# A linear attention and gated MLP kernel: turned queries on GpSimd's DMA queue, the verdict by a product with ones

## The chip, the cores and the metric

The kernel runs on one core of a Trainium2 chip. The core has five engines with a queue of instructions each: TensorE (PE, with its weight loads shown apart as PEld), VectorE (DVE), ScalarE (ACT), GpSimd (POOL) and SyncE (SP), and 16 DMA engines that serve the transfers which SP, ScalarE or GpSimd issue. The metric is the device time of one execution in microseconds; lower is better.

## What is computed

The reference is a gated linear recurrence over 768 steps for 4 batches of 8 heads (head size 48), followed by an MLP whose activation is h·cos(h):

```python
def _attn_ref(q, k, v, a_re, a_im):
    mag = np.sqrt(a_re * a_re + a_im * a_im)
    scale = np.minimum(mag, 0.999) / (mag + 1e-06)
    a_re_n, a_im_n = (a_re * scale, a_im * scale)
    for t in range(S):
        ar, ai = (a_re_n[:, :, t, :, None], a_im_n[:, :, t, :, None])
        new_re = ar * S_re - ai * S_im
        new_im = ar * S_im + ai * S_re
        kv = np.einsum('bhd,bhe->bhde', k[:, :, t], v[:, :, t])
        S_re, S_im = (new_re + kv, new_im)
        y[:, :, t] = np.einsum('bhd,bhde->bhe', q[:, :, t], S_re)

def _moe_ref(x, w_in, w_out):
    h = x @ w_in
    g = h * np.cos(h)
    return (g @ w_out).astype(np.float32)
```

Between the two, the attention output is rearranged to 3072 tokens of 384 numbers; w_in is 384x2048 and w_out 2048x384.

## The kernel before

The 768 steps of a batch are cut into chunks of 128; two chunks make a group, and there are 12 groups. There are two programs in one kernel. `fast_path` assumes things that its data may break (for example decays that stay in a range, gate arguments that a table can take), and keeps records of them in three small tiles, `least`, `odd` and `wide`. At the end `verdict` turns these records into one number, `flag`. Every engine reads the flag and branches: in one arm `general_path` computes everything again, in the other only the last piece of the output is stored (`late["store"]`, issued by ScalarE).

In a group of the fast path, logarithms, powers, phases and sines of the decays come first. `g_stack` (L909) multiplies keys and queries by cosine and sine and stacks both products into `ks` and `qs`; four VectorE multiplies, keys first. `f_transpose` (L921) then turns the stacks so that the head's numbers lie on partitions: VectorE transposes blocks of 32 into `tr`, SP stores `tr` to DRAM (`moved`), and SP loads it back in another order, keys as `kT` in four transfers, queries as `qT` in one. The chunk's scores (`sc`, from kT and qT) are masked into `atm`, its outputs (`yp`) go through DRAM once more to become `xT`, and the MLP follows: `hp` is xT times w_in, ScalarE and VectorE make `gate` from it, and the second product is done in seven half-sized products instead of eight (`products`, with sums in `sum` and `op`; `seventh`, L1160, evicts each one into `ot`, the last group's last quarter into `rest`).

The order of the work is written out by hand up to group 2; after it `weave` (L1213) merges lists of steps by position numbers between 0 and 1, one body for each of groups 2 to 11: products of the group before, scores and outputs of this group, the decays, phases and `keys` of the next group, and `first`, the 96 `hp` matmuls of this group, at the end. The next group's keys and queries are turned while these matmuls run, and its scores stand right behind them on TensorE. TensorE's and GpSimd's instructions are each tied into one chain in the order in which they are written (`chain`); the other queues are ordered by the tile framework from these positions.

GpSimd does little: it loads weights, and from group 4's body on (`guarded`) it waits with a one-element copy (`wait_for`, L1277) for the last gate of the group before, and then loads two pieces of the raw weights again, into one buffer, for VectorE and ScalarE to look at (`guard`, L645).

In the last body `judged` advances the verdict in three steps. The first (L1610 to L1624) reduces the three records on VectorE and writes the two results to DRAM as one line, which SP loads back into one partition; the second (L1626 on) takes the minimum of that line, compares, and has all engines read the flag; the third only fixes TensorE's place.

Of the kernel before, what the change touches and what calls it, by code (L numbers as in the profile page):

```python
# [11 lines left out]
F32 = mybir.dt.float32  # L12
# [475 lines left out]
def fast_path(ctx, tc, q, k, v, a_re, a_im, moe_w_in, moe_w_out, out, least, odd, wide,  # L488
# [417 lines left out]
        special(out=sn, in_=ph, func=AF.Sin, scale=TWO_PI)  # L906
        special(out=cs, in_=cs, func=AF.Sin, scale=-TWO_PI, bias=half_pi_b)

    def g_stack(g, i, n):  # L909
        x = X[g]  # L910
        if i == 0:
            for name in "ks", "qs":
                x[name] = gt.tile([C, G * H, 2, D], F32, tag=name, name=name)
        for name, product in ("ks", "Q"), ("qs", "mag"):
            for a, trig in enumerate(("cos", "sin")):
                vector.tensor_tensor(
                    out=x[name][:, ds(i * H, n * H), a],
                    in0=cut(x[product], i, n).rearrange("p (x d) -> p x d", d=D),
                    in1=cut(x[trig], i, n).rearrange("p (x d) -> p x d", d=D), op=ALU.mult)

    def f_transpose(g, i, n, name):  # L921


        if i == 0:
            X[g][name] = ft.tile([D2, G * H, Q4, 32] if name == "kT" else [D2, Q4, G * H, 32], F32,
                                 tag=name, name=name, bufs=1)
        tr = ft.tile([C, NB, n * H, 32], F32, tag="tr", name="tr")
        turn = vector.transpose(out=tr, in_=X[g][name[0] + "s"][:, ds(i * H, n * H)].rearrange(
            "p x a d -> p x (a d)").rearrange("p x (r b) -> p b x r", b=NB))
        if name == "qT" and "gated" in X[g - 1]:  # L930
            behind(turn, X[g - 1]["gated"])
        moved = rows_d.tile([Q4, D2, n * H, 32], F32, tag="moved", name="moved", bufs=3)
        nc.sync.dma_start(out=moved.rearrange("q (r b) x j -> (q r) b x j", b=NB), in_=tr)
        if name == "kT":
            for q4 in range(Q4):
                nc.sync.dma_start(out=X[g][name][:, ds(i * H, n * H), q4], in_=moved[q4])
        else:
            nc.sync.dma_start(out=X[g][name][:, :, ds(i * H, n * H)],
                              in_=moved.rearrange("q c x j -> c q x j"))

    def f_turn(g, i, name, hh):

# [217 lines left out]
    def seventh(g, p, part):  # L1160


        x, name = X[g], SEVEN[p]
        if p == 0 and part == 0:
            x["sum"] = pm.tile([C, E2], F32, tag="acc", name="sum", bufs=1)
            x["ot"] = [msb.tile([C, DM], F32, tag="ot", name="ot") for _ in range(G)]

        alone = g == NG - 1 and p == 6
        summed = p in (0, 3, 5, 6) and not alone
        if not summed and part == 0:  # L1170
            x["op"] = pm.tile([C, E2], F32, tag="m", name="op", bufs=2)
        ps = x["sum"] if summed else x["op"]
        for j in range(part * HJ // 2, (part + 1) * HJ // 2):
            matmul(ps, lhsT=left(g, name, j), rhs=right[name][:, j],
                   start=(j == 0 and (p == 0 or not summed)),
                   stop=(j == HJ - 1), skip_group_check=summed)
        if part == 0:
            return
        c11, c12, c21, c22 = (x["ot"][i][:, ts(half, E2)] for i in range(2) for half in range(2))
        if g == NG - 1:  # L1180
            c12 = rest
        if p in (0, 3, 5) or p == 6 and not alone:
            late["scalar"] = scalar.mul(out={0: c11, 3: c21, 5: c22, 6: c12}[p], in_=ps, mul=scale)
        if g == NG - 1 and p == 5:
            scalar.mul(out=c12, in_=ps, mul=scale)
        for part_ in {1: [c11], 2: [c21], 4: [c21, c22], 6: [c12] * alone}.get(p, []):
            added = vector.scalar_tensor_tensor(out=part_, in0=ps, scalar=scale,
                                                in1=part_, op0=ALU.mult, op1=ALU.add)
            if alone:
                behind(added, late["read DVE"])  # L1190
            late["vector"] = added
        row = g * G * C
        if g == NG - 1 and p == 1:
            behind(nc.sync.dma_start(out=out[ds(row, C), 0:E2], in_=c11), late["line"])
        elif p == 4:
            put = nc.sync.dma_start(out=out[ds(row + C, C), :], in_=x["ot"][1])
            if g == NG - 1:
                behind(put, late["read SP"])
        elif p == 6 and alone:
            late["store"] = lambda: nc.scalar.dma_start(out=out[ds(row, C), E2:DM], in_=c12)  # L1200
        elif p == 6:
            nc.sync.dma_start(out=out[ds(row, C), :], in_=x["ot"][0])
# [7 lines left out]
    def mixes(g, lo, hi):  # L1210
        return [lambda p=p: mixed(g, p) for p in range(lo, hi)] if g >= PLAIN else []
# [14 lines left out]
    def keys(g):  # L1226

        if not 0 <= g < NG:
            return
        for i, n in spans(g):  # L1230
            yield lambda i=i, n=n: g_trig(g, i, n)
            yield lambda i=i, n=n: (g_stack(g, i, n), p_end(g, i, n))
            for name in "kT", "qT":
                if g >= PEG:
                    yield lambda i=i, n=n, name=name: f_transpose(g, i, n, name)

    def turned(g, i, name):
        return [lambda hh=hh: f_turn(g, i, name, hh) for hh in range(2)]
# [329 lines left out]
    for n in range(2, NG):  # L1568
        weave((mixes(n - 1, 2, 4), 0.0, 0.12), (logs(n + 1), 0.0, 0.02), (chunks(n), 0.0, 0.36),
              (upper[2:] if n == 2 else [], 0.0, 0.2), (products(n - 1, 0, 2 + (n < NG - 1)), 0.0, 0.36),  # L1570
              (prods(n + 1), 0.25, 0.27), (second(n - 1, 1), 0.36, 0.5),
              (products(n - 1, 2 + (n < NG - 1), 7), 0.4, 0.56),
              (phases(n + 1), *((0.472, 0.476) if n == PLAIN else (0.516, 0.524))),
              (keys(n + 1), *((0.5, 0.62) if n == PLAIN else (0.53, 0.64))),
              (last_quarter() if n == PLAIN else [], 0.9, 1.0), (first(n), 0.56, 1.0),
              (mixes(n, 0, 2), 0.9, 1.0), (guarded(n - 1, per) if n > 3 else [], 0.1, 0.9))
    checked = verdict(late, temp)

    def judged():
        late["tensor"] = tail["tensor"]  # L1580
        next(checked, None)

    weave((mixes(NG - 1, 2, 4), 0.0, 0.1), ([judged], 0.05, 0.15),
          (products(NG - 1, 0, 7), 0.0, 1.0), ([judged], 0.58, 0.6), ([judged], 0.76, 0.8))
    assert not guards
    return late
@with_exitstack
def kernel(ctx, tc, q, k, v, a_re, a_im, moe_w_in, moe_w_out, out):
# [16 lines left out]
        tc.add_manual_dep(ins.ins, other.ins.name, mybir.DependencyInfo(  # L1605
            mybir.DependencyClass.NoSync, mybir.DependencyReason.DATA))

    def verdict(late, temp):

        low = keep.tile([D2, 1], F32, name="low")  # L1610
        nc.vector.tensor_reduce(out=low, in_=least, axis=AX.X, op=ALU.min)
        even = keep.tile([C, 1], F32, name="even")
        nc.vector.tensor_reduce(out=even, in_=odd, axis=AX.X, op=ALU.max)
        most = keep.tile([C, 1], F32, name="most")
        nc.vector.tensor_reduce(out=most, in_=wide, axis=AX.X, op=ALU.max)
        nc.vector.tensor_scalar(out=even, in0=even, scalar1=0.0, scalar2=None, op0=ALU.is_le)
        nc.vector.tensor_scalar(out=most, in0=most, scalar1=2.4, scalar2=None, op0=ALU.is_le)
        nc.vector.tensor_tensor(out=even, in0=even, in1=most, op=ALU.mult)
        line_d = scratch.tile([D2 + C], F32, name="line_d")
        behind(nc.sync.dma_start(out=line_d[0:D2], in_=low.rearrange("p o -> (p o)")),  # L1620
               late["x"])
        nc.sync.dma_start(out=line_d[D2:D2 + C], in_=even.rearrange("p o -> (p o)"))
        line = temp("Q")[0:1, 0:D2 + C]
        late["line"] = nc.sync.dma_start(out=line, in_=line_d.unsqueeze(0))  # L1624
        yield
        bad = keep.tile([1, 2], F32, name="bad")  # L1626
        behind(nc.vector.tensor_reduce(out=bad[:, 0:1], in_=line, axis=AX.X, op=ALU.min),
               late["vector"])
        flag = keep.tile([1, 1], I32, name="flag")
        nc.vector.tensor_scalar(out=flag, in0=bad[:, 0:1], scalar1=0.5, scalar2=None,  # L1630
                                op0=ALU.is_lt)
        reads, values = nc.values_load_multi_w_load_instructions(
            flag[0:1, 0:1], min_val=0, max_val=1,
            skip_runtime_bounds_check_because="a comparison gives 0 or 1")
        late["taken"] = values[0]
        for ins in reads:
            name = str(ins.ins.engine).split(".")[-1]
            late["read " + name] = ins
        behind(late["read Activation"], late["scalar"])
        yield  # L1640
        behind(late["read PE"], late["tensor"])
# [36 lines left out]
```

## Time and profile before

| what | value |
|---|---|
| median of 3 timed runs | 655.68 us (655.22 to 656.19) |
| the profiled execution | 653.01 us, of which the span from first to last instruction is 651.2 us |
| granted TensorE clock | 1.000 |
| scores of 384 matmuls (PE sc) | 49.0 us busy, 276 ns mean |
| hp, 1176 matmuls | 252.5 us busy, 375 ns mean |
| stores of turned stacks (moved<-tr) | 20 issues of 768 KB |
| kT loads | 40 issues of 192 KB; shortest, median, longest issue 584, 1323, 2581 ns |
| qT loads | 10 issues of 768 KB; shortest, median, longest issue 804, 1185, 1384 ns |
| SP's queue (q1) | 225,320 packets, 68.51 MB, 45.3% of 16 engines' span |
| GpSimd's queue (q0) | 5,824 packets, 25.50 MB, 11.7% |

A busy time is the time in which the engine had at least one instruction running. Most matmuls are recorded at L687, a helper, so they are told apart by their tiles. A DMA issue's duration is the time that the issuing queue was held, not the transfer's. A group of the steady part takes 50.2 to 51.2 us, of which the 96 hp matmuls are 20.7 us.

### The profile page before, as it was taken

To read this page: it belongs to the slowest core of one execution; us is meant where nothing else is said; L and a number is where in the kernel's file an instruction comes from. 1 tells how busy PE (TensorE), PEld (TensorE's weight loads), DVE (VectorE), ACT (ScalarE), POOL (GpSimd) and SP (SyncE) were. 2 spreads that over 40 slices of the span, in tenths; PEclk is the share of its full clock that TensorE was granted. 3 is DMA by queue.
4 is the path that set the end of the run, shared out by engine and by line. 5 is a ranking of instruction groups with operands and counts; after the bars stand their busy time and mean duration, and the time that the engine had idled before them with its cause. 6 is when DMAs were issued, how large, how long until landed. Compare 5 with 4: busy or idle time off the path is not lost.

```text
span 651.2 us, 10758 instructions
## 1 busy us (share of the span) xinstructions
PE 641.0 (98%) x4075; PEld 576.4 (89%) x4075; DVE 492.0 (76%) x799; ACT 392.8 (60%) x726; POOL 30.9 (5%) x53
## 2 busy tenths in 40 slices
PE   8999999999999999999999999999999999999997
PEld 6888877777999999899899899899899999999996
DVE  6999989888687688786787787876877878862251
ACT  7898687284583593494494485485576476433330
POOL 4010200000000000010010010000000000000000
PEclk9999999999999999999999999999999999999999
DMA  9968755727627656747738737836836843363001
GB/s 249 244 179 203 225 164 123 170 62 182 146 49 182 158 146 148 194 110 167 209 82 191 204 85 167 205 96 151 226 105 146 219 123 98 112 134 120 25 1 31
DMA packets 232920, 94.90 MB, mean 146 GB/s; under 512 B 208701, under 2 KB 221246, under 8 KB 232858
## 3 DMA queue, kind: packets, MB, share of 16 engines
q1 hardware_dynamic: 225320, 68.51, 45.3%
q0 software_dynamic: 5824, 25.50, 11.7%
q8 instruction: 34, 0.56, 0.4%
q10 hardware_dynamic: 1714, 0.11, 0.2%
q14 instruction: 28, 0.23, 0.1%
HBM read 69.28 MB, written 24.81 MB: 144 GB/s over the span
## 4 chain that ended last, share of the span: by engine, by line
PE 92%; ACT 4%; DVE 3%; DMA 0%; issue 0%; SPq 0%; DVEq 0%
PE hp L687 38%; PE op L687 18%; PE sum L687 16%; PE sc L687 6%; PE yp L687 6%; PE sp L687 4%; PE phs L687 2%; PE lgs L687 1%; ACT tan L707 1%; PE yr L687 1%; PE tp L948 1%; ACT rs L707 1%; ACT lg L707 1%; ACT L703 1%; DVE mag L676 1%; DVE atm L676 1%
## 5 line engine op out<-in xcount | busy, mean ns | idle before, releaser
L687 PE MATMUL hp<-xT,w_in 128*128 128x256 f32 (+1 forms) x1176 | 252.5, 375 | 0.0
L687 PEld LDWEIGHTS hp<-xT,w_in 128*128 128x128 f32 x1176 | 219.6, 190 | 30.2 <-issue 0.2
L707 ACT ACTIVATE gate<-hp,half_pi_b 128x512 f32<-128x512 f32 x96 | 66.0, 687 | 118.5 <-PE hp L687 118.5
L687 PE MATMUL op<-w_out,gate 128*128 128x192 f32 (+1 forms) x448 | 100.7, 374 | 0.0
L676 DVE TENSOR_TENSOR gate<-hp,gate 128x512 f32<-128x512 f32 x96 | 65.7, 684 | 45.8 <-ACT junk L676 45.7
L687 PEld LDWEIGHTS op<-w_out,gate 128*128 128x128 f32 x448 | 75.9, 190 | 16.9 <-issue 2.0
L676 ACT ACTIVATE junk<-hp 128x512 bf16<-128x512 f32 x96 | 56.7, 591 | 0.0
L687 PE MATMUL sum<-t_s,s 128*128 128x192 f32 x320 | 56.3, 329 | 0.0
L687 PEld LDWEIGHTS sum<-t_s,s 128*128 128x128 f32 x320 | 52.1, 190 | 1.5 <-issue 1.5
L676 DVE TENSOR_TENSOR atm<-sc,causal 128x512 f32<-128x512 f32 x48 | 32.9, 689 | 23.4 <-PE sc L687 23.4
L687 PEld LDWEIGHTS sc<-qT,kT 96*128 96x128 f32 x384 | 47.4, 192 | 2.3 <-issue 0.6
L687 PE MATMUL sc<-qT,kT 96*128 96x128 f32 x384 | 49.0, 276 | 0.2 <-ACT qT L676 0.2
L676 ACT ACTIVATE ot<-sum 128x192 f32<-128x192 f32 x39 | 12.6, 322 | 53.7 <-PE sum L687 53.4
L676 DVE SCALAR_TENSOR_TENSOR ot<-op,ot 128x192 f32<-128x192 f32 x40 | 13.3, 354 | 38.0 <-PE op L687 36.4
L687 PE MATMUL yp<-atm,v 128*48 128x128 f32 x352 | 33.6, 277 | 0.9 <-ACT Q L707 0.6
L703 ACT ACT_TABLE_LOAD x24 | 30.8, 1283 | 1.2 <-PEq L1662 0.7
L676 ACT COPY yT<-yp 48x512 f32<-48x512 f32 x44 | 25.3, 574 | 7.4 <-PE yp L687 7.0
L687 PE MATMUL yp<-qT,state 96*48 96x128 f32 x304 | 29.7, 272 | 0.0
L687 PE MATMUL sum<-w_out,gate 128*128 128x192 f32 x160 | 29.7, 329 | 0.0
L687 PE MATMUL sp<-v,ks 128*96 128x48 f32 x320 | 29.7, 245 | 0.0
L687 PEld LDWEIGHTS sp<-v,ks 128*96 128x96 f32 x320 | 29.6, 165 | 0.0
L676 ACT CAST tan<-phs 128x384 int32<-128x384 f32 x24 | 11.4, 480 | 29.4 <-PE phs L687 29.4
(147 smaller groups left out, 987.4 us busy)
## 6 DMA issues: line engine op xcount, KB each, us to landing
moved<-tr SPq DMA_DIRECT2D x20, 768.0 KB
raw<-in_moe_w_in_dram POOLq DMA_DIRECT2D x16, 768.0 KB, 5.1
raw<-in_moe_w_out_dram POOLq DMA_DIRECT2D x16, 768.0 KB, 4.6
kT<-moved SPq DMA_DIRECT2D x40, 192.0 KB
qT<-moved SPq DMA_DIRECT2D x10, 768.0 KB
k<-in_k_dram SPq DMA_DIRECT2D x24, 192.0 KB
q<-in_q_dram SPq DMA_DIRECT2D x24, 192.0 KB
v<-in_v_dram SPq DMA_DIRECT2D x24, 192.0 KB
```

The lines of the kernel that those rows point to most:

```text
L676: ins = getattr(self.engine, op)(**kw)
L687: chain(nc.tensor.matmul(out, **kw), "tensor")
L703: chain(nc.scalar.preload_act_table_set(table))
L707: chain(nc.scalar.activation(func=func, **kw))
L948: chain(nc.tensor.transpose(ps[:, h], X[g][name[0] + "s"][:, x0 + h].rearrange("p a d -> p (a d)"), ident), "tensor")
```

## The change

Four things are edited. The loads of `qT` for groups 3 to 11 are issued by GpSimd instead of SP, in GpSimd's chain; with them `keys` is split into smaller steps, so that the keys' stack and transpose are written ahead of the queries' stack, and `p_end` comes last. The guards' positions end at 0.68 instead of 0.9. The verdict's line through DRAM is gone: the per-partition results are multiplied together on VectorE (1 where all is well), summed over partitions by a matmul with ones (`counted`), and the sum compared with 127.5; its second step stands at 0.42 to 0.44 of the last weave instead of 0.58 to 0.6. In the last group VectorE takes the two evictions of product 5 that ScalarE did.

```diff
-    def g_stack(g, i, n):
+    def g_stack(g, i, n, names=("ks", "qs")):
         x = X[g]
-        if i == 0:
-            for name in "ks", "qs":
+        for name in names:
+            product = {"ks": "Q", "qs": "mag"}[name]
+            if i == 0:
                 x[name] = gt.tile([C, G * H, 2, D], F32, tag=name, name=name)
-        for name, product in ("ks", "Q"), ("qs", "mag"):
             for a, trig in enumerate(("cos", "sin")):
...
         else:
-            nc.sync.dma_start(out=X[g][name][:, :, ds(i * H, n * H)],
-                              in_=moved.rearrange("q c x j -> c q x j"))
+            queue = nc.sync if g <= PEG else nc.gpsimd
+            put = queue.dma_start(out=X[g][name][:, :, ds(i * H, n * H)],
+                                  in_=moved.rearrange("q c x j -> c q x j"))
+            if g > PEG:
+                chain(put, "gpsimd")
...
-        if p in (0, 3, 5) or p == 6 and not alone:
+        if g == NG - 1 and p == 5:
+            for out_ in c22, c12:
+                vector.tensor_scalar(out=out_, in0=ps, scalar1=scale, scalar2=None, op0=ALU.mult)
+        elif p in (0, 3, 5) or p == 6 and not alone:
             late["scalar"] = scalar.mul(out={0: c11, 3: c21, 5: c22, 6: c12}[p], in_=ps, mul=scale)
-        if g == NG - 1 and p == 5:
-            scalar.mul(out=c12, in_=ps, mul=scale)
...
         if g == NG - 1 and p == 1:
-            behind(nc.sync.dma_start(out=out[ds(row, C), 0:E2], in_=c11), late["line"])
+            nc.sync.dma_start(out=out[ds(row, C), 0:E2], in_=c11)
...
             yield lambda i=i, n=n: g_trig(g, i, n)
-            yield lambda i=i, n=n: (g_stack(g, i, n), p_end(g, i, n))
+            if g <= PEG:
+                yield lambda i=i, n=n: (g_stack(g, i, n), p_end(g, i, n))
             for name in "kT", "qT":
+                if g > PEG:
+                    yield lambda i=i, n=n, name=name: g_stack(g, i, n, (name[0] + "s",))
                 if g >= PEG:
                     yield lambda i=i, n=n, name=name: f_transpose(g, i, n, name)
+            if g > PEG:
+                yield lambda i=i, n=n: p_end(g, i, n)
...
-              (mixes(n, 0, 2), 0.9, 1.0), (guarded(n - 1, per) if n > 3 else [], 0.1, 0.9))
-    checked = verdict(late, temp)
+              (mixes(n, 0, 2), 0.9, 1.0), (guarded(n - 1, per) if n > 3 else [], 0.1, 0.68))
+    def counted(even):
+
+        ps = pa.tile([1, 1], F32, tag="a", name="good")
+        matmul(ps, lhsT=even, rhs=one_b, start=True, stop=True)
+        return ps
+
+    checked = verdict(late, counted)
...
-          (products(NG - 1, 0, 7), 0.0, 1.0), ([judged], 0.58, 0.6), ([judged], 0.76, 0.8))
+          (products(NG - 1, 0, 7), 0.0, 1.0), ([judged], 0.42, 0.44), ([judged], 0.76, 0.8))
...
         nc.vector.tensor_tensor(out=even, in0=even, in1=most, op=ALU.mult)
-        line_d = scratch.tile([D2 + C], F32, name="line_d")
-        behind(nc.sync.dma_start(out=line_d[0:D2], in_=low.rearrange("p o -> (p o)")),
-               late["x"])
-        nc.sync.dma_start(out=line_d[D2:D2 + C], in_=even.rearrange("p o -> (p o)"))
-        line = temp("Q")[0:1, 0:D2 + C]
-        late["line"] = nc.sync.dma_start(out=line, in_=line_d.unsqueeze(0))
+        nc.vector.tensor_tensor(out=even[0:D2], in0=even[0:D2], in1=low, op=ALU.mult)
         yield
-        bad = keep.tile([1, 2], F32, name="bad")
-        behind(nc.vector.tensor_reduce(out=bad[:, 0:1], in_=line, axis=AX.X, op=ALU.min),
-               late["vector"])
+        good = counted(even)
         flag = keep.tile([1, 1], I32, name="flag")
-        nc.vector.tensor_scalar(out=flag, in0=bad[:, 0:1], scalar1=0.5, scalar2=None,
-                                op0=ALU.is_lt)
+        behind(nc.vector.tensor_scalar(out=flag, in0=good, scalar1=C - 0.5, scalar2=None,
+                                       op0=ALU.is_lt), late["vector"])
```

On the engines' queues this comes out as follows. On SP the nine qT loads and the three transfers of the verdict are missing, and nothing else changes its order: both stores of turned stacks still stand ahead of the four kT loads. On GpSimd the qT loads of groups 3 and 4 come behind the first weights, and from the body of group 4 on each stands behind the wait for a gate and the two weight loads. On VectorE the keys' transpose stands ahead of the last query multiply; the queries' transpose keeps its place behind the first gate product of the group before. On TensorE the product `good` stands behind the last group's third product, and all else keeps its order.

More of the change, by code (lines that the diff above doesn't have):

```diff
@@ L1606, in behind, with verdict @@
             mybir.DependencyClass.NoSync, mybir.DependencyReason.DATA))
-    def verdict(late, temp):
+    def verdict(late, counted):
         low = keep.tile([D2, 1], F32, name="low")
```

## The prediction, made before the changed kernel ran

> **What bounds the kernel now.** I read four views: busy time by engine, the table by stretches, the timeline around one hand-over of turned queries, and the timeline of the end.
>
> ```profile
> PE 641.0 (98%) x4075; PEld 576.4 (89%) x4075; DVE 492.0 (76%) x799; ACT 392.8 (60%) x726; POOL 30.9 (5%) x53
> ```
> TensorE works 641.0 of 651.2 us, so an edit can only win out of the 10.2 us in which it doesn't, or lose by making it wait. The stretches say where these lie:
>
> ```profile
> 305.80:356.10 50.30, 50.30 (x331) 46.98 (x330) 39.74 (x64) 31.77 (x60) 1.85 (x3) 1.00 0.65 162
> 508.00:560.00 52.00, 51.85 (x349) 48.22 (x348) 40.71 (x69) 32.05 (x61) 1.78 (x3) 1.00 0.47 127
> 628.20:646.50 18.30, 18.30 (x113) 18.04 (x111) 4.24 (x14) 2.48 (x7) 0.00 (x0) 1.00 0.08 20
> 646.50:651.20 4.70, 0.03 (x1) 0.00 (x0) 0.36 (x1) 0.00 (x0) 0.00 (x0) 1.00 0.11 31
> ```
> The columns are stretch, length, busy PE, PEld, DVE, ACT, POOL, granted clock, DMA share, GB/s. Inside a group of the steady part nothing idles; after the last product 4.7 us pass without TensorE. The remaining idle time is ahead of 154 us, in code that the diff leaves alone.
>
> The steady part is full, but by how much? Timeline lines of one group, and DMA by single microseconds (same columns as above):
>
> ```profile
> 314.25 4.79 SPq L936 DMA_DIRECT2D kT<-moved  x4
> 319.16 1.22 SPq L938 DMA_DIRECT2D qT<-moved  x1
> 326.33 1.06 PE L687 MATMUL sc<-qT,kT 96*128 96x128 f32 x8
> ```
> ```profile
> 323.00:324.00 1.00, 1.00 (x7) 0.87 (x6) 0.93 (x3) 0.06 (x1) 0.00 (x0) 1.00 1.03 262
> 324.00:325.00 1.00, 1.00 (x6) 0.90 (x5) 0.93 (x3) 1.00 (x2) 0.00 (x0) 1.00 0.25 59
> ```
> The queries are the last data that the scores need. Their 768 KB run until after 324 us, the last semaphore increment comes at 325.35, and the scores start at 326.33. From the semaphore records of the nine groups 3 to 11 the margins between landing and scores are 1.11, 1.14, 0.55, 0.98, 0.48, 0.76, 0.97, 0.14 and 1.09 us (mean 0.80). At 528 us the queries land at 528.34 and the scores start at 528.48, already slightly held. So TensorE's full row hangs on nine transfers arriving with under a microsecond to spare.
>
> The end:
>
> ```profile
> 632.08 0.33 SPq L1622 DMA_DIRECT2D line_d<-even  x1
> 638.54 0.25 SPq L1624 DMA_DIRECT2D Q<-line_d  x1
> 641.72 0.38 DVE L1627 TENSOR_REDUCE bad<-Q 1x1 f32<-1x224 f32 x1 [2.54 <-DMA Q<-line_d]
> 646.64 0.36 DVE L676 SCALAR_TENSOR_TENSOR rest<-op,rest 128x192 f32<-128x192 f32 x1 [2.05 <-PE op L687]
> 647.03 1.17 ACTq L1200 DMA_DIRECT2D out_dram<-rest  x1
> ```
> The verdict goes through DRAM: 6.46 us until the write is answered, 3.2 us for the read. The flag is there at 642.27, ScalarE branches at 642.83 and has its first instruction in the arm at 645.58 (sequencer records). Its store waits for VectorE's last sum until 647.03. So the verdict has about 1.4 us to spare.
>
> [...] Here 16 weight loads from GpSimd have a median issue of 0.75 us and a maximum of 1.04, beside a busy VectorE[...]. [...] 2.75 us from branch to arm on ScalarE, 2.8 on VectorE (646.7 to 649.52).
>
> **The change part by part**, against the profiled execution's 653.01 us (span 651.2 and 1.8 around it). The runs shown have a median of 655.68, 2.67 higher; the change in time is carried over to that.
>
> *qT on GpSimd's queue, nine times.* SP issues it now at 319.16, behind four kT issues (4.79 us), and its packets begin at 321.5, when kT's are through. Its source has landed at 317.37. GpSimd would issue at about 317.4, take 0.75 us as for a weight load of the same 768 KB, and have first packets 1.45 us after issue (as these loads do), about 318.9. Ahead of it on GpSimd are, per group, a one-element copy that waits for the last gate product (done by 329) and two weight loads, the second issued at 339.67 when ScalarE has used the first; all are some 25 us older than the next turned queries, and the earlier guard positions (0.68) keep them so. Nothing queued behind it is urgent: the next copy waits for a later gate anyway. When does the pair land? From 317 to 324.3 the DMA engines are busy without a hole, with kT for about 4 us and qT for about 3. If they only share, both end at 324.3 as before: gain nothing, kT later but harmless. If the 128-byte kT packets leave room for 2 KB ones, up to 1.5 us sooner (estimate: half of qT's 3 us hidden). If sharing makes kT's small packets slower, later. I take 0.7 sooner, which doubles the margin; kT, now through at 321.99, is then as late as qT. In the profiled execution this removes about 0.1 us in all (528 us).
>
> *Stacks split.* VectorE turns the keys one multiply (0.95 us) sooner, in front of the last query product. But SP issues both stores ahead of kT, and the second waits for the queries' transpose, whose place is unchanged: 0.
>
> *Verdict by a product.* Removes three SP transfers, VectorE's 0.38 us reduction, and the round trip; adds a 1x1 product between two products at about 636 us, and a 96x1 multiply (0.15) under them. No such matmul is in the trace; bounds: 0.06 us (the pitch of small yp products) to 0.3 (that, and the 0.2 us which op x8 loses after yp: 1.50 against 1.30). I take 0.2 lost. The flag is ready about 636.6 instead of 642.27, and ScalarE is in the arm near 640. VectorE now waits for that product in order, but its next sum is due only at 638.8.
>
> *VectorE takes two evictions of ScalarE* (0.32 each) at 641.4; it has nothing due until 643.97: 0.
>
> *The end.* ScalarE's store issue lasted 1.17 us where SP's issue of the same 96 KB lasted 0.34. [...] SP's last wait before that landing ended 649.58, on VectorE's own arrival in its arm at 649.52; against the landing at 650.21 at most 0.63 is won. I take 0.3. Sum in the profiled execution: -0.1 + 0.2 - 0.3 = -0.2, bounds -0.7 and +0.3.
>
> *What the timed runs hold besides.* They spread over 1 us and lie 2.2 to 3.2 us above the profiled one, with the same fixed TensorE work at clock 1.00. Waits of TensorE are the natural place: nine margins of 0.14 to 1.14 us, and one verdict with 1.4 to spare, all hung on DMA latency. If the transfers land 1.0 us later than in the profiled execution, the nine waits sum to 2.1 us. I take 1.8 of the 2.67 as such waits and removed; bounds 0 and 2.67. Total -2.0: **653.7**, own range 652.4 to 654.4.
>
> **Rivals.**
> *Nothing to win* (0.27): the gap between timed and profiled is a constant of measuring. For: the profiled execution shows hardly one wait. Then only -0.2 stays: 655.5, or 655.0 to 656.0.
> *The shared DMA engines make the pair later* (0.16): kT, until now alone, lands after qT used to. Place: the first scores of each group. With a slip of 1.0 the nine waits sum to 2.1 us, with 1.5 to 6.3. Slower than before by over 0.2% from a slip of about 0.9. Taking 1.0: 655.68 - 0.2 + 2.1 = 657.6. For: the engines were saturated, GpSimd adds its latency. Against: qT's packets can begin 2.6 us sooner.
>
> **How the numbers follow.** Forecast 0.57, no change 0.27, slower 0.16. About 0.2% (1.3 us) is what a measurement of this kernel can tell from no change. The range 652.4 to 657.0 takes in the forecast, the first rival and the edge of the second.
>
> **What would show it.** Right: GpSimd issues qT within 0.5 us of its source's landing, the last of kT and qT lands by 324.7 in that group's terms, no DMA read of a verdict, ScalarE in the arm about 7 us before its store. Wrong: kT landing later than qT did before with TensorE waiting ahead of the scores; a store issue still of 1.17 us; timed and profiled runs as far apart as now.

## The result and the profile after

The changed kernel takes 660.23 us (median of 6 runs, 659.58 to 660.94) where the kernel before takes 655.72 (6 runs, 654.71 to 656.41): a ratio of 1.007 [1.0057, 1.0083], slower. The profiled execution took 660.43 us, with the clock at 1.00.

The page of the changed kernel: the span, busy time by engine, SyncE's DMA queue, and the two groups of the scores' instructions, whose last column is the idle time just before them and what ended most of it.

```profile
span 658.6 us, 10763 instructions
...
PE 643.7 (98%) x4077; PEld 575.9 (87%) x4077; DVE 492.1 (75%) x801; ACT 392.5 (60%) x724; POOL 40.3 (6%) x62
...
q1 hardware_dynamic: 221462, 61.43, 47.6%
...
L687 PEld LDWEIGHTS sc<-qT,kT 96*128 96x128 f32 x384 | 46.8, 192 | 10.1 <-DMA qT<-moved 6.0
L687 PE MATMUL sc<-qT,kT 96*128 96x128 f32 x384 | 49.6, 277 | 5.5 <-DMA kT<-moved 4.8
```

The same lines of the kernel before:

```profile
q1 hardware_dynamic: 225320, 68.51, 45.3%
...
L687 PEld LDWEIGHTS sc<-qT,kT 96*128 96x128 f32 x384 | 47.4, 192 | 2.3 <-issue 0.6
L687 PE MATMUL sc<-qT,kT 96*128 96x128 f32 x384 | 49.0, 276 | 0.2 <-ACT qT L676 0.2
```

Two things are to be seen. TensorE now stands idle ahead of the scores (5.5 us against 0.2), and the DMA that ends most of it is that of kT or qT. And q1 moves 7 MB less than before (61.43 against 68.51, the nine qT loads have left it), yet its packets take more time, 47.6% of 16 engines' span against 45.3%.

The hand-over that the prediction showed, in the changed kernel. The timeline (start, length, engine, line, operation; in brackets what the engine waited for):

```profile
316.82 0.33 SPq L933 DMA_DIRECT2D moved<-tr  x1
317.24 5.19 SPq L936 DMA_DIRECT2D kT<-moved  x4
321.55 0.69 POOL L939 DMA_DIRECT2D qT<-moved  x1 [29.01 <-DMA moved<-tr]
329.82 1.13 PE L687 MATMUL sc<-qT,kT 96*128 96x128 f32 x8 [0.47 <-DMA kT<-moved]
```

and the stretches ahead of these scores (stretch, length, busy PE, PEld, DVE, ACT, POOL, clock, DMA share, GB/s):

```profile
324.00:326.00 2.00, 2.00 (x11) 1.77 (x10) 0.50 (x1) 1.27 (x3) 0.00 (x0) 1.00 1.00 207
326.00:328.00 2.00, 2.00 (x11) 1.77 (x10) 1.71 (x5) 1.21 (x3) 0.00 (x0) 1.00 1.07 199
328.00:330.00 2.00, 1.53 (x8) 1.05 (x7) 0.69 (x1) 0.68 (x3) 0.00 (x0) 1.00 0.39 53
```

The scores were due at 329.35 (0.47 earlier), and the DMA engines are still moving kT and qT after 328 (a share of 0.39 until 330). By the semaphore records the last of kT lands at 329.7, qT at 329.4.

The end, on the timeline:

```profile
643.79 0.19 PE L687 MATMUL good<-one_b,even 128*1 128x1 f32 x2
643.91 2.87 PE L687 MATMUL op<-t_a,gate 128*128 128x192 f32 x16
644.02 0.14 DVE L1638 TENSOR_SCALAR flag<-good 1x1 int32<-1x1 f32 x1 [2.31 <-PE good L687]
...
654.62 0.36 DVE L676 SCALAR_TENSOR_TENSOR rest<-op,rest 128x192 f32<-128x192 f32 x1 [1.98 <-PE op L687]
655.01 0.39 ACTq L1204 DMA_DIRECT2D out_dram<-rest  x1
```

The flag is ready 11 us before the last store, and that store's issue lasts 0.39 us instead of 1.17. So the end does what it should, and the loss lies in the groups.

### The profile page after: what moved, and what is told of

Its sections match the earlier page's. It is cut to its first block, busy times and chain, and to the rows that moved or that the text cites. A ratio compares the mean times of both kernels' runs of the same rounds, so it can differ in the third digit from the quotient of the medians.

```text
span 658.6 us, 10763 instructions
## 1 busy us (share of the span) xinstructions
PE 643.7 (98%) x4077; PEld 575.9 (87%) x4077; DVE 492.1 (75%) x801; ACT 392.5 (60%) x724; POOL 40.3 (6%) x62
## 3 DMA queue, kind: packets, MB, share of 16 engines
q1 hardware_dynamic: 221462, 61.43, 47.6%
## 4 chain that ended last, share of the span: by engine, by line
PE 73%; DMA 9%; DVE 8%; ACT 4%; SPq 4%; issue 2%; POOL 0%; DVEq 0%
PE hp L687 22%; PE op L687 17%; PE sum L687 13%; DMA kT<-moved 7%; PE sc L687 6%; PE yp L687 6%; PE sp L687 4%; DVE tr L676 3%; SPq L936 3%; PE phs L687 2%; DVE ks L676 2%; PE lgs L687 1%; DVE qs L676 1%; DVE tan L676 1%; PE yr L687 1%
```

## Experiments

All ratios are to the kernel before on the same chip. Two measures recur. The *hold* is how far the first scores of a group start behind the end of the `hp` products, against the normal order (they start 0.16 us before that end), summed over groups 3 to 11. The *packet time* is the mean time of one DMA packet in the trace: 128 bytes for kT, over the whole trace; 192 bytes for the loads of q, k, v and decays, from 60 us on (over the whole trace the slow kernels' loads have 0.3 to 0.5 ns more, the others' at most 0.1). Holds, landings and packet times come from one profiled execution of each kernel.

### The parts of the change

First a plain repeat of the kernel before, and the change in three pieces.

> The kernel before, unchanged, for a second profile on the chip of these runs. If the profiled execution of before was a lucky one and the timed ones hold waits of TensorE ahead of the scores, this one should show DMA holds of some 0.3 us in several of the groups 3 to 11 and a span of about 653 to 654 us. If the 2.7 us between timed and profiled are a constant, it shows a span of about 651 us and a time of 653 again.

This second profiled execution took 653.97 us, span 652.2, again without a hold. The profile of before was thus a fair one, though at the quick end: the timed runs beside it have a median of 655.35 us (27 runs, 653.74 to 657.22). Of what was expected, the first case has the span right and the holds wrong. The second, a constant, is contradicted: 653.97 lies within the timed runs, and in every later kernel the profiled execution is itself one of the timed runs (660.43 in the changed kernel, whose runs go from 659.58 to 660.94).

The queue alone, without the split, the verdict or the evictions:

```diff
-            nc.sync.dma_start(out=X[g][name][:, :, ds(i * H, n * H)],
+            queue = nc.sync if g <= PEG else nc.gpsimd
+            put = queue.dma_start(out=X[g][name][:, :, ds(i * H, n * H)],
...
+            if g > PEG:
+                chain(put, "gpsimd")
...
-              (mixes(n, 0, 2), 0.9, 1.0), (guarded(n - 1, per) if n > 3 else [], 0.1, 0.9))
+              (mixes(n, 0, 2), 0.9, 1.0), (guarded(n - 1, per) if n > 3 else [], 0.1, 0.68))
```

> Kernel before with only the qT loads of groups 3 to 11 on GpSimd's queue (and the guards' positions that keep them behind the weight loads). Theory (the two queues share the DMA engines badly, the last kT lands after qT, TensorE waits nine times): slower than before by 4 to 6 us, all of it in front of the scores. Rival (the split of the stacks delays the queries' transpose): no loss, within 1 us of before.

Measured: 654.00 us (22 runs), 0.9985 [0.9975, 0.9994]. The edit under suspicion doesn't cost by itself, it wins a little: the theory of 4 to 6 us was wrong.

The changed kernel with `qT` put back on SyncE's queue, and the kernel before with only the verdict and the evictions:

```diff
-            queue = nc.sync if g <= PEG else nc.gpsimd
-            put = queue.dma_start(out=X[g][name][:, :, ds(i * H, n * H)],
...
+            nc.sync.dma_start(out=X[g][name][:, :, ds(i * H, n * H)],
...
```

> The changed kernel with only the qT loads back on SP; split stacks, guards, product verdict and moved evictions stay. Theory (queue): equal to before or some 0.5 us faster (tail), kT landed 2 us ahead of qT again. Rival (split): still 3 us or more slower than before.

> Kernel before with only the verdict by a product with ones, its earlier place and the two evictions on VectorE. Both theories: 0.4 to 0.7 us faster than before, from a store issue of about 0.4 us instead of 1.17, less 0.2 us for the product; more (up to 2 us) only if the DRAM round trip of the verdict is late in the timed runs of before.

Measured: 658.53 us (6 runs), 1.0064 [1.0043, 1.0086], and 658.23 us (6 runs), 1.005 [1.0034, 1.0065]. All three kernels with the new verdict are slow. But the loss isn't at the verdict. The page of the kernel with the new verdict alone, SyncE's queue and the scores:

```profile
q1 hardware_dynamic: 225062, 68.51, 53.0%
...
L687 PE MATMUL sc<-qT,kT 96*128 96x128 f32 x384 | 49.6, 277 | 2.8 <-DMA qT<-moved 1.6
```

The same 68.51 MB as before, in 258 packets fewer, take 53.0% of the DMA engines' span instead of 45.3%. The packet time of kT is 19.1 ns instead of 13.0, that of the loads 18.1 instead of 15.6. In the first 50 us the loads have 19.6 instead of 15.6 already, hundreds of us before the first changed instruction runs. In the changed kernel the packet times are 18.3 and 17.8, and kT's in group 2, whose qT stays on SyncE, is 19.9; in the kernel with the queue alone they are 13.6 and 15.6.

### A theory of addresses

What can an edit at the end change from the start? Where data lie. The verdict's diff drops a small tile:

```diff
-        bad = keep.tile([1, 2], F32, name="bad")
```

Its 8 bytes take a slot of 32 in the pool `keep`, which is laid out ahead of the others. The built programs give the address of each tile in SBUF:

| tile | before | changed | verdict edited, 32 bytes put back |
|---|---|---|---|
| `re`, first buffer | 68992 | 68960 | 68992 |
| `k`, first buffer | 75136 | 75104 | 75136 |
| `kT`, in groups with a transpose | 121344 | 121312 | 121344 |

Addresses in DRAM stay. Theory: 32 bytes less, and kT's pieces start off multiples of 128; they move more slowly, and land past the margin. Four kernels test it. The changed kernel with 32 unused bytes in `keep`, and the kernel before with 32, 64 and 96 unused bytes more (8, 16, 24 numbers):

```diff
+        keep.tile([1, 8], F32, name="pad")
         flag = keep.tile([1, 1], I32, name="flag")
```

> The changed kernel with 32 unused bytes put where the removed tile bad stood, so that every later SBUF tile is back at its address of before (multiples of 64 bytes instead of 32 more). New theory (the 32 byte shift slows every transfer into SBUF, and that costs the time): 653.2 to 654.5 us, that is 1 to 2 us faster than before; first kT transfer back to 4.0 us from issue to landing. Rival (something in the product verdict or the split itself, or its sum with the other queue): still 658 us or more.

> Kernel before with 32 unused bytes more ahead of all large SBUF tiles, nothing else. New theory: 3 us slower than before, kT transfers 5.0 us from issue to landing instead of 4.0. Rival (addresses don't matter): same time as before.

> Kernel before with 64 unused bytes more ahead of all large SBUF tiles. If what counts is a multiple of 64 bytes: same time as before. If it is a multiple of 128 or more (the tiles of before start at multiples of 128): slower by 1 to 3 us.

> Kernel before with 96 unused bytes more, so that tiles start at 96 above a multiple of 128, as in the changed kernel (32 less). If the place within 128 bytes decides: kT packets of about 19 ns as in tail_alone (13.0 in before, 16.0 with 32 more, 15.7 with 64 more) and a time some 3 us above before. If only being off a multiple of 128 counts: about 16 ns.

The fifth is the kernel before with kT alone off by 32 bytes (its tile 128 bytes wider, so that all others keep multiples of 128):

```diff
...
+                X[g][name] = ft.tile([D2, G * H * C + 32], F32, tag=name, name=name, bufs=1)[
+                    :, ds(8, G * H * C)].rearrange("p (x q j) -> p x q j", q=Q4, j=32)
...
```

> Kernel before with only the tile kT started 32 bytes further (its 128-byte pieces then lie across 64-byte bounds); all other tiles stay at multiples of 64 bytes. If the small pieces of kT carry the loss: most of the 3 us, with kT's transfers slower and the first loads of the kernel as before. If it is spread over all loads: under 1 us slower.

And a sixth removes the slot and nothing else: the kernel before, its two numbers of `bad` kept in `low`'s slot, so that every tile lies where the changed kernel has it and every instruction is that of before.

```diff
-        low = keep.tile([D2, 1], F32, name="low")
+        lows = keep.tile([D2, 3], F32, name="low")
+        low = lows[:, 0:1]
...
-        bad = keep.tile([1, 2], F32, name="bad")
+        bad = lows[0:1, 1:3]
```

> The kernel before, with its two numbers of `bad` put into the tile of `low` (12 instead of 4 bytes per partition, in a slot of 32 either way), so that only the slot of 32 bytes goes and every later tile starts 32 bytes lower, as in the changed kernel; every instruction stays. Theory of addresses: 658 to 660 us, 1.004 to 1.006 of before, waits of TensorE on DMA ahead of the scores. If the sign of the shift decides how much slower kT's packets are, their mean is near 19 ns as in the three kernels with the slot gone; if those owed the 19 to the chip they ran on, or to their own instructions, near 16 as in the kernels with 32, 64 and 96 bytes more. Rival, that one of the change's instructions is the cause and the shift upwards only resembles it: as before, 655.9.

| kernel | us, runs | ratio to before | kT packet, ns | load packet, ns |
|---|---|---|---|---|
| before, profiled | | | 13.0 | 15.6 |
| changed | 660.23, 6 | 1.007 [1.0057, 1.0083] | 18.3 | 17.8 |
| changed, 32 put back | 653.41, 11 | 0.9962 [0.994, 0.9983] | 13.4 | 15.7 |
| before, slot removed (-32) | 659.13, 4 | 1.0057 [1.0037, 1.0077] | 18.7 | 18.1 |
| before +32 | 659.51, 11 | 1.0054 [1.0029, 1.0078] | 16.0 | 18.1 |
| before +64 | 658.65, 13 | 1.004 [1.0023, 1.0058] | 15.7 | 15.9 |
| before +96 | 659.11, 12 | 1.0051 [1.0036, 1.0066] | 15.8 | 17.3 |
| before, kT alone +32 | 658.84, 18 | 1.0042 [1.0025, 1.0059] | 15.8 | 15.9 |

At +64 the kernel loses as well, so a multiple of 64 isn't enough. The slot's removal is shown to be the cause: with it alone the kernel before is about as slow as the pieces with the verdict, and with the slot put back the changed kernel is faster than before. Its whole size isn't accounted for: the 32 bytes cost the kernel before 1.0057, but the changed kernel 1.0108 (1.007 over 0.9962, an estimate). A part may be the queue: with the slot gone the holds are 3.8 us where qT is back on SyncE and 6.4 where it is on GpSimd, though the times of these two, 1.0064 and 1.007, don't tell them apart.

The page of the kernel before with the slot removed:

```profile
span 657.2 us, 10758 instructions
...
PE 642.1 (98%) x4075; PEld 575.2 (88%) x4075; DVE 491.5 (75%) x799; ACT 392.6 (60%) x726; POOL 34.4 (5%) x53
...
q1 hardware_dynamic: 225320, 68.51, 53.0%
...
L687 PE MATMUL sc<-qT,kT 96*128 96x128 f32 x384 | 49.6, 278 | 3.8 <-DMA qT<-moved 2.5
```

Packets and bytes are those of before to the last one, and their share is 53.0% instead of 45.3%. Its timeline in the group where the prediction found the smallest margin:

```profile
520.56 6.51 SPq L936 DMA_DIRECT2D kT<-moved  x4
527.20 0.90 SPq L938 DMA_DIRECT2D qT<-moved  x1
...
534.18 1.02 PE L687 MATMUL sc<-qT,kT 96*128 96x128 f32 x7 [1.44 <-DMA qT<-moved]
```

Before, the same lines stood at 516.35 (6.25 us), 522.73 and 528.48; by the semaphore records qT lands 6.85 us after its issue's start, where before it was 5.62.

The changed kernel with 32 bytes put back, page and the timeline of the hand-over:

```profile
span 651.7 us, 10763 instructions
...
q1 hardware_dynamic: 221462, 61.43, 41.6%
...
L687 PE MATMUL sc<-qT,kT 96*128 96x128 f32 x384 | 49.0, 276 | 0.6 <-DMA kT<-moved 0.3
```

```profile
314.72 4.54 SPq L936 DMA_DIRECT2D kT<-moved  x4
318.77 0.69 POOL L939 DMA_DIRECT2D qT<-moved  x1 [28.28 <-DMA moved<-tr]
326.65 1.06 PE L687 MATMUL sc<-qT,kT 96*128 96x128 f32 x8
```

The same 221,462 packets as in the changed kernel fall from 47.6% to 41.6% of a shorter span, kT's issues take 4.54 us instead of 5.19, and the wait in brackets is gone.

That the loss arises at kT is shown by the kernel that moves kT: it loses nearly as much as the shifts of everything, with the loads as fast as before. The tiles laid out behind kT, qT and `tr`, moved by 128 bytes in it, but kT lands 1.55 us later, while `tr`'s second store ahead of it lands 0.1 later and qT follows kT after 3.06 us instead of 3.55 (means of groups 3 to 11). The profile page of it:

```profile
q1 hardware_dynamic: 225320, 68.51, 48.4%
...
L687 PE MATMUL sc<-qT,kT 96*128 96x128 f32 x384 | 49.7, 278 | 3.0 <-DMA qT<-moved 2.2
```

What sets the slow starts apart can be read from the landings of kT's four transfers. kT is written in pieces of 128 bytes, 512 apart, and each transfer starts 128 bytes behind the one before. Before, kT's tile starts at a multiple of 256 (121344), and no piece crosses such a multiple. At +32, +64 and +96 every piece of the second and fourth transfer crosses one; at -32, which is 224 above a multiple of 256, every piece of the first and third. The landings differ in the same way (against the kernel before, counted from the start of the group's `hp` products, means of groups 3 to 11; each group's kT packets cut into quarters in order of start):

| kernel | transfers whose pieces cross | transfers 1 to 4 land later by, us | packet time by quarter, ns |
|---|---|---|---|
| before | none | | 13.0, 13.0, 13.0, 13.0 |
| before, slot removed (-32) | 1, 3 | 1.01, 0.90, 1.28, 1.13 | 13.0, 20.6, 20.5, 20.7 |
| before +32 | 2, 4 | 0.30, 0.97, 0.92, 1.58 | 13.0, 13.3, 18.2, 19.5 |
| before +64 | 2, 4 | 0.19, 1.02, 0.90, 1.59 | 13.0, 13.1, 18.6, 18.1 |
| before +96 | 2, 4 | 0.17, 0.91, 0.90, 1.55 | 13.0, 13.1, 17.8, 19.5 |

The delay grows by 0.4 to 1.0 us at each transfer that crosses; at the others by at most 0.3, or it shrinks. In this transfers 1 and 3, which start 256 bytes apart, go together in every row, and so do 2 and 4; neighbours, 128 apart, don't where the tile was moved. That is a pattern of these five kernels; what causes it isn't shown. My expectation that the place within 128 bytes decides failed: -32 and +96 have the same place within 128 bytes, but differ in which transfers cross. The slow packets begin one quarter behind the first transfer that crosses. That gives three slow quarters at -32 and two at the others, and so a mean of 18.7 ns against 15.8. It is no higher price: the last of kT lands 1.13 us later at -32, and 1.55 to 1.59 later at the upward shifts. The expected 5.0 us from issue to landing of kT's first transfer came with the slot removed (5.06 against 4.09), not at +32 (4.31), where that transfer doesn't cross.

Nor is it shown which packets are slow. The median is 13 ns in every kernel; 33% of kT's packets took longer with the slot removed and 15% at the upward shifts, where half of the pieces cross. And no chip is known to have run both a -32 kernel and an upward shift, so a part that belongs to the chip isn't excluded. A kernel with 224 bytes more, run beside these, would tell: it has the starts of -32.

The loads write pieces of 192 bytes one after the other. From a multiple of 64 two of four cross a multiple of 256, before and at +64 (15.6 and 15.9 ns); from the other starts three of four (17.3 to 18.1 ns).

### The change with its addresses mended

The pieces with the new verdict again, each with the 32 bytes put back:

> Kernel before with the verdict by a product and the two moved evictions, and 32 unused bytes in place of the tile bad. Theory (the loss of tail_alone was all address): 0.3 to 1.0 us faster than before, end after the last product about 4.05 us instead of 4.7, good costing 0.2. Rival (a part of that loss belongs to the product verdict): slower than before.

> The changed kernel with qT back on SP and the 32 bytes filled. Theory: as tail_realigned within 0.4 us, since SP issues the queries' store ahead of all kT loads and so the earlier keys' transpose wins nothing; what after_realigned has over this is the queue, about 1 us. Rival (the split brings the gain): about 653.4 like after_realigned.

Measured: 655.03 us (22 runs), 0.9983 [0.9969, 0.9997], and 655.09 us (22 runs), 0.9984 [0.9974, 0.9994]. With the queue's 0.9985 the pieces add up to 0.9969; the whole has 0.9962 with an interval that holds it. The split adds nothing that these runs can tell.

The profiled executions of these two were 655.21 and 655.29 us, close to their medians, and show what such an execution holds. Waits of TensorE in the kernel with the verdict alone (us in all, times, longest):

```profile
PE hp L687 <- DVE ks L676: 1.3, 1, 1.3
PE sc L687 <- DMA qT<-moved: 0.7, 1, 0.7
```

and in the kernel with split and verdict:

```profile
PE hp L687 <- DMA xT<-x: 1.0, 1, 1.0
PE sc L687 <- DMA qT<-moved: 0.9, 1, 0.9
```

Both first waits stand at the same place (from 457.6 and 457.9 us on, ahead of the first `hp` product of a group, which reads xT); the profile of before has neither. The releaser named in the first is doubtful, since `hp` doesn't read `ks`; the same wait in the second kernel is put down to the transfer of xT. So single transfers are late in these two executions; that qT's place on SyncE is the reason isn't shown.

## Why the prediction was wrong

**Where it failed.** The step is *Verdict by a product*: "Removes three SP transfers, VectorE's 0.38 us reduction, and the round trip; adds a 1x1 product". It counted instructions and put at nothing, without a word, what the diff shows beside them: a tile that is no longer allocated. That had a price of 1.0057 [1.0037, 1.0077] by itself, some 3.3 us (659.13 against 655.83) where the step had 0.2. How it comes about, from the semaphore records of groups 3 to 11 (us after the start of the group's `hp` products; the scores are due at 20.72):

| kernel | kT landed, mean | qT landed, mean | last of both, mean | holds in all |
|---|---|---|---|---|
| before | 16.38 | 19.93 | 19.93 | 0.1 |
| before, slot removed | 17.51 | 21.07 | 21.07 | 4.6 |
| changed | 21.26 | 20.47 | 21.26 | 6.4 |
| changed, 32 put back | 19.72 | 19.03 | 19.72 | 0.5 |

kT's 6144 packets in a group are 384 for each of 16 DMA engines on average; 5.7 ns more on each (18.7 - 13.0) are 2.2 us more of packet time. kT's landing shows half of that, 1.13 us; where the rest is hidden isn't shown. qT stands behind kT and lands 1.14 us later. The margins that the prediction listed, 0.14 to 1.14 us with a mean of 0.80, were right and could not hold that.

**Where the 7.4 us of span went** (658.6 - 651.2), with the other two kernels:

| place | changed | slot removed | changed, 32 put back |
|---|---|---|---|
| until the first scores (23.5 us before) | +0.7 | +0.7 | +0.4 |
| holds of groups 3 to 11 | +6.3 | +4.5 | +0.4 |
| `good` between two products | +0.2 | 0 | +0.2 |
| from the last product's end on (4.70 before) | -0.6 | +0.2 | -0.6 |
| the rest | +0.8 | +0.6 | +0.1 |

**The rival that came near.** "The shared DMA engines make the pair later" named the place (the first scores of each group, with kT landing last) and the size of the price: the pair slipped 1.33 us and TensorE was held 6.4, where its margins give 4.8 for an even slip of 1.33 (estimate). That it came so near is luck, for its cause was not the main one: with addresses as before, sharing made the pair 0.21 us sooner (19.72 against 19.93), and with the slot gone and nothing shared the holds are 4.6 already. Its chance of 0.16 was no measure of the risk that decided.

**qT on GpSimd, issue and queue.** Predicted: issue at the landing of its source, 0.75 us long, the pair 0.7 sooner. The issue takes 0.69, but starts at 321.55 in the changed kernel where the source landed at 320.6, almost 1 us later, and 0.6 in other groups, so the mark "within 0.5 us" was missed. The other mark, landing by 324.7, which is 19.1 us after that group's start of `hp`, was missed as well: 21.2 in the changed kernel, and 19.8 with the 32 bytes put back. In the mended kernel qT itself is 0.9 us sooner (19.03 against 19.93), but kT 3.3 later, because the two didn't alternate piece by piece: in the changed kernel, between 324 and 326 us, the trace has 101 of qT's packets and 4 of kT's, and the last of kT's four transfers moves only from 327 on. (On this queue qT goes in packets of 4096 bytes, not in the 2 KB ones that the estimate of 1.5 us assumed.) qT is 12 pieces for each engine on average (768 KB in pieces of 4096 bytes on 16 engines); why they went nearly in one run isn't shown. The gain was 0.2 us in landing, not 0.7.

**Split: 0.** Right. In the changed kernel the keys' store is issued 0.93 us sooner (4.48 against 5.41 us after the start of `hp`), the queries' 0.14 later, and kT behind both 0.14 later (8.79 against 8.65).

**The product: 0.2 lost.** Right: `good` starts at 643.79, and the next product at 643.91 instead of 643.70 (2.60 after its forerunner, the pitch of the others). That is 0.21.

**Evictions on VectorE: 0.** Right as to waits: at 649.42 and 649.69 it had nothing else due.

**The end: -0.3, at most -0.63.** The direction was right, the size too small: from the last product's end to the span's end 4.06 us instead of 4.70, so -0.64, at that bound. And 4.70 was the quickest of its kind. Over all profiled executions the end takes 4.70 to 5.64 us in the eight with the old verdict and 4.05 to 4.28 in the six with the new one, and the store's issue 1.17 to 1.51 us against 0.39 in all six. So a bound that was read from one execution was too tight.

What makes the store's issue 0.8 us shorter isn't shown. In the changed kernel ScalarE branches at 644.73 and is in the arm at 647.67, 7 us before its store. The trace records two instruction reads of 8192 bytes 0.92 and 1.02 us after the branch (643.76 and 643.85 before, 645.65 and 645.75 in the changed kernel). One more such read begins 0.67 us after the start of the long issue (at 647.70) and 0.66 after that of the short one (at 655.67), so these reads don't tell the two issues apart.

**The timed runs hold waits: -1.8.** Not shown for the kernel before: no execution of it near its median was profiled. Its rival, a constant of measuring, is contradicted (see the second profile of before). Two near relatives, profiled at their medians, hold 1.9 to 2.0 us of waits that the profile of before lacks, but only 0.7 and 0.9 of these stand ahead of scores, where the prediction had put them. Another part can lie at the end, which took up to 0.9 us more than the 4.70 in other executions with the old verdict.

With the addresses mended the whole change gives 653.41 us, 0.3 from the forecast of 653.7, ten of its eleven runs within 1 us; against the kernel before on the same chip that is -2.6 where -2.0 was forecast. This agreement is in part luck. The largest term, 1.8, isn't shown, and the sum of -0.2 for profiled executions isn't either: the mended kernel was profiled at 653.44, the kernel before at 653.01 and 653.97.

## What to carry to other kernels

Dropping a tile of 8 bytes moved the large tiles behind it by 32 here, and kT landed 1.13 us later and qT behind it 1.14, where the margins had a mean of 0.80. Where a transfer of 128-byte pieces has about a microsecond to spare, compare the addresses in the two built programs before adding up instructions. When a kernel is slow in places far from what was edited, look for the mean time of a DMA packet in untouched code: here it told a change of layout (loads at 18.1 ns instead of 15.6 with the new verdict alone) from a change of order (15.6 with the queue alone). Pad small tiles, as was done here (653.41 us instead of 660.23), so that the aligned starts of large ones don't hang on them; a pool of their own behind the large ones should do the same, but wasn't tried.

## What was not expected of the hardware

In these kernels the start of a tile in SBUF set the time of small DMA pieces. 128-byte pieces took 13.0 to 13.6 ns in the mean from a multiple of 256 and 15.7 to 19.1 ns from the four other starts that were measured, and each transfer of kT whose pieces cross a multiple of 256 landed 0.4 to 1.0 us further behind; 192-byte pieces took 15.6 to 15.9 ns from multiples of 64 and 17.3 to 18.1 from the three others. Two transfers on two queues didn't share the DMA engines evenly: one of 4096-byte packets ran nearly alone for 2 us (101 packets to 4) while one of 128-byte packets stood still. Still open are what causes this, why only 15 to 37% of kT's packets are slow when half of the pieces cross, why the 32 bytes cost the changed kernel more than the kernel before, and what the executions of the kernel before at its median hold.
